# A cross network on one core: four staggered groups, batched tails and a row-major last layer in place of two interleaved groups

## The chip, the cores and the metric

The kernel runs on one core of a Trainium2 chip. That core has a matrix engine (TensorE, PE in the profile, with its weight loads as PEld), a vector engine (VectorE, DVE), a scalar engine (ScalarE, ACT), GpSimd (POOL), and SyncE (SP), which here only issues transfers to the core's 16 DMA engines. Matrix products land in PSUM (8 banks of 128 x 512 fp32); everything else lives in SBUF. The metric is the device time of one execution in microseconds. The kernel before was run three times: 513.07, 513.36 and 513.94 us, a median of 513.36.

## The reference

```python
B, F, D, L = 16384, 26, 16, 6
Din = min(F * D, 1024)            # 416
x = x0                            # x0: [16384, 416] bf16
for l in range(L):
    proj = jnp.einsum('bd,de->be', x, ws[l]) + bs[l]
    x = x0 * proj + x
return x
```

Six layers; each multiplies all 16384 rows by a 416 x 416 matrix, adds a bias, multiplies by the first input and adds the layer's input. The rows are independent of each other; the layers of one row follow each other.

## The kernel before, in words

**Layout.** The rows are cut into 8 groups of 2048 (`NG`, `GC`), a group into four chunks of 512 (`G_CH`, `CH`). Data is kept transposed: features on the partitions, rows along the free axis. 416 features are three tiles of 128 and a tail of 32. A group's three tiles are 128 x 2048 each; its tail is folded to 128 x 512, the four chunks below each other in strips of 32 partitions.

**One job** is one layer of one group. Its main tile i needs for each chunk three full products (128 x 128 weights, `emit_full`, L504) and one product of the 32 tail rows, which is row-tiled: four chunks at once in four strips of the array (`emit_k32`, L526 and L528). The tail of the output needs column-tiled products for the three main tiles (`emit_tail_cp`, L539, four chunks at once in four strips of 32 columns) and one 128 x 128 product with a block-diagonal weight `wbd` (`emit_tail_bd`, L559). In the order of a job the tile forms are full, rows, rows, full, full, rows, columns, block-diagonal. Tile 1 is begun with its row products and ended with its full ones (`k32_first`).

**Evacuation.** For each bank ACT adds the bias and writes bf16 to a staging tile `tmpw` (L420, 128 x 512). DVE multiplies a whole tile of 128 x 2048 by x0 (L738) and adds the old x (`emit_add`, L704), one addition held back behind the next multiply.

**Order.** `units` runs pairs of groups: groups 0 and 1 alternate through all six layers, then 2 and 3, and so on (`R = 2`). Each engine has its program written out by hand, with counters on semaphores. The first job of a layer waits for `sem_dve` of the same group's layer before, so that one other job lies between the two.

**Loads.** SP transposes x0 from DRAM into SBUF, three tiles and `Tbuf` for the tail, for each group (L238, L243, L253). For groups 2 to 7 a burst of four small products (`emit_x3init`, L485) copies the tail from `Tbuf` through PSUM into its folded form; groups 0 and 1 do that in their first job (L618).

**Outputs.** Groups 0 to 5 are written to a DRAM scratch `x6T` (L272, L275), transposed from there into `ost` (L296) and stored (L285). Groups 6 and 7 are transposed by PE at the end (L656, L658), copied out of PSUM by ACT (L449) and DVE (L773) and stored from SP (L346) and ACT (L436).

Of the kernel before, what the change touches and what calls it, by code (L numbers as in the profile page):

```python
# [3 lines left out]
P = 128  # L4
CH = 512

ACT_F = mybir.ActivationFunctionType
ALU = mybir.AluOpType
BF16 = mybir.dt.bfloat16
FP32 = mybir.dt.float32  # L10


def bass_standalone__cross_network_dcn__recsys_kernel(
# [8 lines left out]
    NMT = 3  # L22
    TAIL = D - NMT * P
    assert TAIL == 32, "kernel specialised for D = 416"
    Q = 4
    G_CH = 4
    GC = G_CH * CH
    assert B % GC == 0
    NG = B // GC
    R = 2 if NG % 2 == 0 else 1  # L30
    NR = NG // R
    NSLOT = 2 * R if NR > 1 else R
    KT = CH // P
    T0 = P - TAIL

    NBANK = 8
    NTW = 3
    NTS = 2
    NOST = 2
    GFIN = NG - 1  # L40
    TD_GROUPS = set(g for g in range(min(NG, 2)))
    N_WARM = 24

    x6T = nc.dram_tensor("x6T_scratch", [NG, D, GC], BF16, kind="Internal")

    wm = [[nc.alloc_sbuf_tensor(f"w_{l}_{t}", [P, D], BF16) for t in range(NMT)] for l in range(L)]
    w3 = [nc.alloc_sbuf_tensor(f"w3_{l}", [P, D], BF16) for l in range(L)]
    wbd = [nc.alloc_sbuf_tensor(f"wbd_{l}", [P, P], BF16) for l in range(L)]
    bias_bf = nc.alloc_sbuf_tensor("bias_bf", [P, 4, L], BF16)
    bias_f = nc.alloc_sbuf_tensor("bias_f", [P, 4, L], FP32)  # L50
    ident = nc.alloc_sbuf_tensor("ident", [P, P], BF16)
    x0T = [[nc.alloc_sbuf_tensor(f"x0T_{s}_{t}", [P, GC], BF16) for t in range(NMT)] for s in range(NSLOT)]
    x03 = [nc.alloc_sbuf_tensor(f"x03_{s}", [P, CH], BF16) for s in range(NSLOT)]
    xb = [[[nc.alloc_sbuf_tensor(f"x_{s}_{k}_{t}", [P, GC], BF16) for t in range(NMT)] for k in range(2)]
          for s in range(NSLOT)]
    xb3 = [[nc.alloc_sbuf_tensor(f"x3_{s}_{k}", [P, CH], BF16) for k in range(2)] for s in range(NSLOT)]
    Tb = nc.alloc_sbuf_tensor("Tbuf", [P, GC], BF16)
    tmpw = [nc.alloc_sbuf_tensor(f"tmpw_{i}", [P, GC], BF16) for i in range(NTW)]
    tmps = [nc.alloc_sbuf_tensor(f"tmps_{i}", [P, CH], BF16) for i in range(NTS)]
    ost = [nc.alloc_sbuf_tensor(f"ost_{i}", [P, KT, D], BF16) for i in range(NOST)]  # L60
    psum = nc.alloc_psum_tensor("ps", [P, NBANK * CH], FP32)

    sem_w = [nc.alloc_semaphore(f"sem_w{l}") for l in range(L)]
    sem_w0m = nc.alloc_semaphore("sem_w0m")
    sem_bias = nc.alloc_semaphore("sem_bias")
    sem_x0 = [nc.alloc_semaphore(f"sem_x0_{s}") for s in range(NSLOT)]
    sem_g0 = [nc.alloc_semaphore(f"sem_g0_{t}") for t in range(NMT)]
    sem_T = nc.alloc_semaphore("sem_T")
    sem_pe = nc.alloc_semaphore("sem_pe")
    sem_act = nc.alloc_semaphore("sem_act")  # L70
    sem_dve = nc.alloc_semaphore("sem_dve")
    sem_dm = nc.alloc_semaphore("sem_dm")
    sem_scr = nc.alloc_semaphore("sem_scr")
    sem_otr = [nc.alloc_semaphore(f"sem_otr{i}") for i in range(NOST)]
    sem_out = [nc.alloc_semaphore(f"sem_out{i}") for i in range(NOST)]
    sem_pool = nc.alloc_semaphore("sem_pool")
    sem_poolw = nc.alloc_semaphore("sem_poolw")
    sem_wbd = nc.alloc_semaphore("sem_wbd")
    sem_pet = nc.alloc_semaphore("sem_pet")
    sem_cpa = nc.alloc_semaphore("sem_cpa")  # L80
    sem_cpd = nc.alloc_semaphore("sem_cpd")
    sem_fin = nc.alloc_semaphore("sem_fin")
    sem_fin2 = nc.alloc_semaphore("sem_fin2")

    def slot_of(g):
        r, q = divmod(g, R)
        return (r % 2) * R + q if NR > 1 else q

    units = []
    for r in range(NR):  # L90
        for l in range(L):
            for q in range(R):
                g = r * R + q
                units.append(("job", g, l))
    for g in range(NG):
        if g in TD_GROUPS:
            continue
        idx = units.index(("job", g, 0))
        units.insert(max(idx - 1, 0), ("x3init", g, 0))

    banks = []
    eunits = []
    main_list = []
    small_list = []
    x3init_bank = {}
    x3init_eu = {}
    job_banks = {}
    job_eus = {}

    def add_eunit(kind, g, l, i, j, nb, ring, rk=None):  # L110
        eu = len(eunits)
        lst = main_list if ring == "w" else small_list
        if rk is None:
            rk = len(lst)
            lst.append(eu)
        else:
            lst[rk] = eu
        e = dict(kind=kind, g=g, l=l, i=i, j=j, first_bank=len(banks), last_bank=len(banks) + nb - 1,
                 ring=ring, rk=rk, ring_wait=(kind != "main1" or j == 0))
        eunits.append(e)  # L120
        return eu

    def add_x3init(g):
        eu = add_eunit("x3init", g, 0, None, None, 1, "s")
        x3init_bank[g] = len(banks)
        x3init_eu[g] = eu
        banks.append(dict(kind="x3init", g=g, l=0, i=None, j=0, eu=eu))

    for u in units:
        if u[0] == "x3init":  # L130
            add_x3init(u[1])
            continue
# [669 lines left out]
```

## Time and profile before

| what | value |
|---|---|
| runs | 513.07, 513.36, 513.94 us |
| span of the profiled execution | 511.6 us |
| its own device time beside the span | not listed apart; the median of the runs is 1.8 us above the span |
| mean granted TensorE clock | 0.995 |
| DMA | 53.91 MB in 134147 packets, mean 105 GB/s |
| ACT waiting for PE (L420 on L528) | 107.4 us in 96 waits |
| DVE waiting for ACT (L738 on L420) | 128.1 us in 95 waits |
| SP waiting for the output staging and scratch | 35.0 us on `out_dram<-ost`, 16.2 us on `ost<-x6T_scratch` |

The profile's page gives the busy time of each engine, then the span in 40 slices with the busy share in tenths, then the chain of work that ended last, and the costliest groups of instructions. A row of the timeline has the start in us, the length, the engine, the line of the kernel, the operation, output and inputs with their shapes, and the count of merged instructions. Matrix products are pipelined: each is listed with some 0.38 us although the next starts 0.22 us later, so spacings are read from starts, not from lengths. Tiles are named without their buffer numbers, so `x_1_0` stands for all tiles of that kind.

### The profile page before, as it was taken

Reading aid. Unit: us, or ns where it says so; the run is one execution under the profiler, and the core shown is the slowest. Engines: PE = TensorE matmul, PEld = TensorE weight load, DVE = VectorE, ACT = ScalarE, POOL = GpSimd, SP = SyncE. Lnnn points to the kernel's source line nnn. Section 1 sums busy time; section 2 is a strip of 40 time slices with the busy share of each in tenths; the row PEclk is TensorE's granted clock in tenths of the full one; section 3 lists DMA queues with packets and bytes.
Section 4 is the critical chain, followed back from the end, with each engine's and each line's share of the span. In section 5 each row is a group of like instructions: output and inputs, shape, how many; then the busy total and the mean of one; then the engine's idle time right before and its main releaser. Section 6 shows DMA issues by size and latency. Waiting matters only on the chain.

```text
span 511.6 us, 7778 instructions
## 1 busy us (share of the span) xinstructions
PE 485.9 (95%) x3069; PEld 198.8 (39%) x3118; DVE 376.9 (74%) x430; ACT 381.9 (75%) x646; POOL 9.5 (2%) x36
## 2 busy tenths in 40 slices
PE   5899999999999999999999999999999999999992
PEld 2333343343334334343433433343343343434352
DVE  0167787787788778778787877877887787787795
ACT  1467787787878778787877878787787777878782
POOL 1020200000000000000000000000000000000000
PEclk9999999999999999999999999999999999999998
DMA  9769700000667799000569579000277660000008
GB/s 168 153 150 206 142 2 0 1 1 1 176 168 233 159 209 190 1 0 2 163 156 247 136 200 215 15 2 1 57 218 217 184 168 0 1 1 0 1 2 266
DMA packets 134147, 53.91 MB, mean 105 GB/s; under 512 B 111584, under 2 KB 131808, under 8 KB 134112
## 3 DMA queue, kind: packets, MB, share of 16 engines
q1 hardware_dynamic: 128252, 51.29, 41.9%
q10 hardware_dynamic: 5860, 2.14, 1.8%
q8 instruction: 24, 0.39, 0.3%
q14 instruction: 11, 0.09, 0.0%
HBM read 2.56 MB, written 23.86 MB: 52 GB/s over the span
## 4 chain that ended last, share of the span: by engine, by line
PE 89%; DVE 3%; issue 2%; DMA 2%; ACT 2%; SPq 1%; DVEq 0%; ACTq 0%
PE ps L504 74%; PE ps L539 7%; PE ps L528 6%; PE ps L526 2%; DMA x0T_2<-in_x_dram 2%; ACT tmpw L420 2%; SPq L243 1%; DVE tmpw L743 1%; DVE x_0_1 L704 0%; PE ps L485 0%; DVE x_0_2 L704 0%; DVE x_1_1 L773 0%; DVE x_0_0 L704 0%; PE ps L656 0%; DVE tmpw L738 0%
## 5 line engine op out<-in xcount | busy, mean ns | idle before, releaser
L420 ACT ACTIVATE tmpw<-ps,bias_f 128x512 bf16<-128x512 f32 x576 | 343.7, 698 | 107.4 <-PE ps L528 107.4
L738 DVE TENSOR_TENSOR tmpw<-tmpw,x0T_2 128x2048 bf16<-128x2048 bf16 x47 | 57.6, 1225 | 51.9 <-ACT tmpw L420 51.9
L738 DVE TENSOR_TENSOR tmpw<-tmpw,x0T_1 128x2048 bf16<-128x2048 bf16 x47 | 57.6, 1226 | 48.2 <-ACT tmpw L420 48.2
L738 DVE TENSOR_TENSOR tmpw<-tmpw,x0T_0 128x2048 bf16<-128x2048 bf16 x47 | 57.3, 1219 | 28.6 <-ACT tmpw L420 28.1
L504 PE MATMUL ps<-x_1_0,w_0 128*128 128x512 bf16 x287 | 74.0, 380 | 3.3 <-issue 3.2
L504 PE MATMUL ps<-x_1_1,w_1 128*128 128x512 bf16 x288 | 73.9, 379 | 0.0
L504 PE MATMUL ps<-x_1_2,w_2 128*128 128x512 bf16 x288 | 73.9, 379 | 0.0
L504 PE MATMUL ps<-x_0_0,w_0 128*128 128x512 bf16 x192 | 49.4, 380 | 2.6 <-issue 2.6
L504 PE MATMUL ps<-x_0_1,w_1 128*128 128x512 bf16 x192 | 49.3, 379 | 0.0
L504 PE MATMUL ps<-x_0_2,w_2 128*128 128x512 bf16 x192 | 49.3, 379 | 0.0
L504 PEld LDWEIGHTS ps<-x_1_1,w_1 128*128 128x128 bf16 x288 | 28.2, 98 | 34.0
L504 PEld LDWEIGHTS ps<-x_1_2,w_2 128*128 128x128 bf16 x288 | 28.2, 98 | 34.0
L504 PEld LDWEIGHTS ps<-x_1_0,w_0 128*128 128x128 bf16 x288 | 25.9, 98 | 36.1 <-issue 10.2
L420 ACT ACTIVATE tmps<-ps,bias_f 128x512 bf16<-128x512 f32 x48 | 33.9, 705 | 0.0
L704 DVE TENSOR_TENSOR x_0_0<-tmpw,x_1_0 128x2048 bf16<-128x2048 bf16 (+1 forms) x27 | 29.7, 1099 | 0.0
L704 DVE TENSOR_TENSOR x_0_1<-tmpw,x_1_1 128x2048 bf16<-128x2048 bf16 (+1 forms) x27 | 29.7, 1099 | 0.0
L704 DVE TENSOR_TENSOR x_0_2<-tmpw,x_1_2 128x2048 bf16<-128x2048 bf16 (+1 forms) x27 | 29.7, 1099 | 0.0
L504 PE MATMUL ps<-x0T_0,w_0 128*128 128x512 bf16 x95 | 27.0, 402 | 2.8 <-DMA w_2<-in_ws_dram 1.4
L504 PE MATMUL ps<-x0T_1,w_1 128*128 128x512 bf16 x95 | 26.2, 399 | 3.2 <-DMA x0T_1<-in_x_dram 3.2
L504 PEld LDWEIGHTS ps<-x_0_2,w_2 128*128 128x128 bf16 x192 | 18.8, 98 | 22.7
L504 PEld LDWEIGHTS ps<-x_0_1,w_1 128*128 128x128 bf16 x192 | 18.8, 98 | 22.7
L504 PEld LDWEIGHTS ps<-x_0_0,w_0 128*128 128x128 bf16 x192 | 17.5, 98 | 23.8 <-issue 6.8
(204 smaller groups left out, 393.9 us busy)
## 6 DMA issues: line engine op xcount, KB each, us to landing
out_dram<-ost SPq DMA_DIRECT2D x25, 416.0 KB, 3.4
x6T_scratch<-x_0_0 SPq DMA_DIRECT2D x6, 512.0 KB
x6T_scratch<-x_0_1 SPq DMA_DIRECT2D x6, 512.0 KB
x6T_scratch<-x_0_2 SPq DMA_DIRECT2D x6, 512.0 KB
w_1<-in_ws_dram SPq DMA_DIRECT2D x6, 104.0 KB
w_2<-in_ws_dram SPq DMA_DIRECT2D x6, 104.0 KB
w_0<-in_ws_dram SPq DMA_DIRECT2D x5, 104.0 KB
out_dram<-x_1_0 SPq DMA_DIRECT2D x1, 416.0 KB, 2.7
```

The source lines that it names most:

```text
L243: sp.dma_start_transpose(x0T[s][t][:, :], x0[0:GC, t * P:(t + 1) * P]).then_inc(sem_g0[t], 16)
L420: act.activation(dst, src, ACT_F.Identity, bias=bias_ap, scale=1.0).then_inc(sem_act, 1)
L504: ins = pe.matmul(bank_ap(nb_of[(i, j)]), wm[l][t][:, ecols], xin[t][:, j * CH:(j + 1) * CH], start=(t == 0 and not k32_first), stop=last,)
L526: pe.matmul(bank_ap(nb_of[(i, j)]), lhsT, rhs, start=True, stop=False, tile_position=tp)
L528: pe.matmul(bank_ap(nb_of[(i, j)]), lhsT, rhs, start=False, stop=True, tile_position=tp).then_inc(sem_pe, 1)
L539: ins = pe.matmul(bank_ap(n, j * TAIL, (j + 1) * TAIL), wm[l][t][:, ecols], xin[t][:, j * CH:(j + 1) * CH], start=(t == 0 and not bd_first ...
L704: dve.tensor_tensor(o_ap, t_ap, i_ap, ALU.add).then_inc(sem_dve, 1)
L738: dve.tensor_tensor(tw[:, :], tw[:, :], x0T[s][i][:, :], ALU.mult).then_inc(sem_dm, 1)
L743: dve.tensor_tensor(tw[:, cols], tw[:, cols], x0T[s][i][:, cols], ALU.mult).then_inc(sem_dm, 1)
```

## The change

The kernel is written anew around a small recorder (`Program`): each instruction is added with the tiles that it reads and writes, and the recorder works out the semaphore waits. What is done on the chip changes in these parts:

- **Order.** A table `order` runs up to four groups at staggered layers: (0,5), (1,4), (2,3), (3,2), then (4,0), (1,5) and so on, as (group, layer). It ramps up from group 0 alone and down to group 7 alone.
- **Tiles in pairs.** Main tiles go in pairs: full products of one, its row products, the row products of the next, its full products. Pairs run across jobs.
- **Tails in batches.** Tails of up to four jobs are computed together (`cuts`, `tails`). The block-diagonal product becomes four column-tiled ones.
- **Evacuation.** ACT evicts two banks at once where they lie beside each other; DVE multiplies and adds halves of 1024 columns, adds right behind their multiplies.
- **Group 0** is loaded row-major by plain transfers and transposed by PE; the biases too. The other groups' tails reach their folded form by small transfers inside SBUF.
- **Outputs** of groups 0 to 6 are transposed by DMA from SBUF into `ost`, without the DRAM scratch.
- **The last layer of group 7** is computed row-major: x is the stationary operand and the weights move. Its x0 is loaded row-major beforehand (`load_last`), the layer's input is transposed by PE (`to_rows`), the bias is a product with a row of ones.

On PE, one steady job and a half of before, from the middle of the program. L504 are full products, L528 and L526 row products, L539 the column-tiled tail, L559 the block-diagonal product:

```order
303 L528 MATMUL ps<-x_2_1,w_3 128x512 x4
304 L539 MATMUL ps<-x_1_0,w_0 32x512 x4
305 L539 MATMUL ps<-x_1_1,w_1 32x512 x4
306 L539 MATMUL ps<-x_1_2,w_2 32x512 x4
307 L559 MATMUL ps<-x_2_1,wbd 128x512
308 L504 MATMUL ps<-x_1_0,w_0 128x512 x4
309 L504 MATMUL ps<-x_1_1,w_1 128x512 x4
310 L504 MATMUL ps<-x_1_2,w_2 128x512 x4
311 L528 MATMUL ps<-x_3_1,w_3 128x512 x4
312 L526 MATMUL ps<-x_3_1,w_3 128x512 x4
```

And of the changed kernel, with four tails in a row and the pairs behind them. L402 are full products, L414 row products, L427 and L432 the tail:

```order
129 L427 MATMUL ps<-x_4,wm 32x512 x12
130 L432 MATMUL ps<-x_4,wbd 32x512 x4
131 L427 MATMUL ps<-x,wm 32x512 x12
132 L432 MATMUL ps<-x_7,wbd 32x512 x4
137 L402 MATMUL ps<-x,wm 128x512 x12
138 L414 MATMUL ps<-x_7,w_5 128x512 x4
139 L414 MATMUL ps<-x_0,w_4 128x512 x4
140 L402 MATMUL ps<-x,wm 128x512 x24
141 L414 MATMUL ps<-x_0,w_4 128x512 x8
142 L402 MATMUL ps<-x,wm 128x512 x24
```

The column-tiled rows stood behind every third tile and now stand once in four jobs; between them twelve full products of one pair join the twelve of the next.

On SP, the output of group 0 before (DRAM scratch, then four transposes of a chunk each, with the stores between):

```order
36 L272 DMA x6T_scratch<-x_0_0 128x2048 [waits sem_dve]
37 L272 DMA x6T_scratch<-x_0_1 128x2048 [waits sem_dve]
38 L272 DMA x6T_scratch<-x_0_2 128x2048 [waits sem_dve]
39 L275 DMA x6T_scratch<-x_0_0 4x32x512 [waits sem_dve]
40 L296 DMA_TRANSPOSE ost<-x6T_scratch 128x4x416 [waits sem_scr]
41 L296 DMA_TRANSPOSE ost<-x6T_scratch 128x4x416
42 L285 DMA out_dram<-ost 128x4x416 [waits sem_otr0]
43 L296 DMA_TRANSPOSE ost<-x6T_scratch 128x4x416 [waits sem_otr0,sem_out0]
```

The output of group 1 in the changed kernel, and the loads of group 6 behind it:

```order
37 L524 DMA_TRANSPOSE ost<-x 128x16x128 [waits sem_out,sem_dve]
38 L524 DMA_TRANSPOSE ost<-x 128x16x128 [waits sem_dve] x2
39 L529 DMA_TRANSPOSE ost<-x_6 128x4x32 x4
40 L535 DMA out_dram<-ost 128x16x416 [waits sem_ot]
41 L295 DMA_TRANSPOSE x_1<-in_x_dram 128x2048 x3
42 L298 DMA_TRANSPOSE Tb<-in_x_dram 128x2048 [waits sem_x03_0]
```

Scratch writes and reads are gone; three large transposes and four small ones read from the x tiles in SBUF. On DVE, in the changed kernel, the first add that writes a set read by such a transpose (job (3,2), tile 0) waits for all seven:

```order
149 L370 TENSOR_TENSOR tw<-tw,x_2 128x1024 [waits sem_act] x2
150 L375 TENSOR_TENSOR x<-tw,x 128x1024 [waits sem_dve] x2
151 L370 TENSOR_TENSOR tw<-tw,x_3 128x1024 [waits sem_act] x2
152 L375 TENSOR_TENSOR x<-tw,x 128x1024 [waits sem_ot,sem_dve]
153 L375 TENSOR_TENSOR x<-tw,x 128x1024 [waits sem_dve]
```

Before, the x buffers of a slot alternated, and no add between two jobs waited on a transfer from SBUF; now six such adds do.

The diff, cut to its core:

```diff
-            for q in range(R):
-                g = r * R + q
-                units.append(("job", g, l))
+    NX0, NXS, NX3, NTW, NTS = 5, 6, 8, 4, 5
+    order = [(0, 0), (0, 1), (1, 0), (0, 2), (1, 1), (2, 0), (0, 3), (1, 2), (2, 1), (3, 0),
+             (0, 4), (1, 3), (2, 2), (3, 1), (0, 5), (1, 4), (2, 3), (3, 2), (4, 0), (1, 5),
+             (2, 4), (3, 3), (4, 1), (5, 0)]
+    order += [(NG - 1 - g, L - 1 - l) for g, l in reversed(order)]
+    cuts = [1, 2, 3, 4, 4, 4, 4, 4, 4, 4, 4, 4, 3, 2]
...
+    def load_group(g):
+        for t in range(NT):
+            add("sp", lambda h, t=t: h.dma_start_transpose(
+                x0s[s][:, t * GC:(t + 1) * GC], x0[rows, t * P:(t + 1) * P]), ...)
+        add("sp", lambda h: h.dma_start_transpose(Tb[:, :], x0[rows, D - P:D]), ...)
+        for j in range(NJ):
+            add("sp", lambda h, q=q, j=j: h.dma_start(x0s[s][q, XW:XW + CH], Tb[P - T32:P, j * CH:(j + 1) * CH]), ...)
...
+    def evacuate(g, l, i, banks, js, step):
+            add("act", lambda h, a=a, w=w, b0=b0: h.activation(
+                tw[r][:, a * CH:(a + w) * CH], psum[:, b0 * CH:(b0 + w) * CH], ACT_F.Identity,
+                bias=bias[:, i, l:l + 1], scale=1.0), ...)
+        for a in range(js[0], js[-1] + 1, step):
+            add("dve", ... ALU.mult), release=True)
+            add("dve", ... ALU.add), hold=True)
...
-                    pe.matmul(bank_ap(n), wbd[l][:, :], xin3[:, :], start=False, stop=True).then_inc(sem_pe, 1)
+    def tails(batch):
+        for (g, l), b in zip(batch, bs_):
+            for t in range(NT):
+                for j in range(NJ):
+                    add("pe", ... wm[l][:, t, NT * P:D], src(t, j, j + 1), tile_position=(0, j * T32))
+            for j in range(NJ):
+                add("pe", ... wbd[l][:, j * T32:(j + 1) * T32], s3, tile_position=(0, j * T32))
...
-                sp.dma_start(x6T[g, i * P:(i + 1) * P, :], xl[i][:, :]).then_inc(sem_scr, 16)
-                sp.dma_start_transpose(ost[os_][:, :, :], x6T[g, :, j * CH:(j + 1) * CH]).then_inc(sem_otr[os_], 16)
+    def output(g):
+        for t in range(NT):
+            add("sp", lambda h, t=t: h.dma_start_transpose(
+                ost[:, :, t * P:(t + 1) * P], xs[s][:, t * GC:(t + 1) * GC]), lane="ot", batch=g)
+        for j in range(NJ):
+            add("sp", lambda h, j=j, q=q: h.dma_start_transpose(
+                ost[:, j * KK:(j + 1) * KK, NT * P:D], x3s[s3][q, :]), lane="ot", batch=g)
+        add("sp", lambda h: h.dma_start(rows.rearrange(pat, **kw), ost...), lane="out", batch=g)
+        free_x.append(s)
...
+    def transposed_chunk(j):
+        for t in range(NT + 1):
+            for k in range(KK):
+                add("pe", ... h.transpose(psum_t(b)[:, c], x0n[:, j, k, t * P:(t + 1) * P], ident[:, :]))
+        for t in range(2):
+            add("act", ... x0s[s][:, cols(t, j)] from psum_t(ba))
+        add("dve", ... x0s[s][:, cols(2, j)] from psum_t(bb))
...
+    def nat_full(kk, j, b, first):
+        for t in range(NT):
+            add("pe", lambda h, t=t: h.matmul(bank(b, n=D), xcol(t, j, kk), wm[l][:, t, :], ...))
+    def nat_mul(kk, j, b):
+        add("act", lambda h: h.activation(o, bank(b, n=D), ACT_F.Copy), ...)
+        add("dve", lambda h: h.tensor_tensor(o, o, x0v, ALU.mult), ...)
+    def nat_store(kk, j0, j1, lane):
+        add("sp", lambda h: h.dma_start(dst, on[:, j0:j1, kk, :]), ...)
```

More of the change, by code (lines that the diff above doesn't have):

```diff
@@ L57, in bass_standalone__cross_network_dcn__recsys_kernel @@
[L57 to L65, printed above, removed]
@@ L777 @@
+    to_rows(1, bka)
+    for j in range(NJ):
+        nat_add(2, j)
+    nat_store(2, 0, NJ, "o7_2")
+    nat_rows(3, bkb, True)
+    for j in range(NJ):
+        nat_full(3, j, bkb[j], False)
+        nat_mul(3, j, bkb[j])
+        nat_add(3, j)
+        if j % 2 == 1:
+            nat_store(3, j - 1, j + 1, f"o7_3_{j}")
+    pr.emit()
 _INS = ['x0', 'ws', 'bs']
```

1287 lines of the change are left out of this document (611 added, 676 removed).

## The prediction

> **What bounds the kernel now.** I read the page's busy shares and slices first, then its chain of waits, then the timeline of PE for one steady job and for both ends.
>
> ```profile
> span 511.6 us, 7778 instructions
> PE 485.9 (95%) x3069; PEld 198.8 (39%) x3118; DVE 376.9 (74%) x430; ACT 381.9 (75%) x646; POOL 9.5 (2%) x36
> PE   5899999999999999999999999999999999999992
> PE 89%; DVE 3%; issue 2%; DMA 2%; ACT 2%; SPq 1%; DVEq 0%; ACTq 0%
> ```
>
> PE is busy in every slice but the first and the last, and 89% of the chain that ends last is PE. So time is gained by taking work or pauses from PE's stream, or by shortening the two ends. A stretch of PE's timeline (start, length, operation, count) shows one job of the steady state, group 3, layer 3:
>
> ```profile
> 207.06 0.39 PE L528 MATMUL ps<-x_2_1,w_3 32*128 32x512 bf16 x4
> 207.38 0.40 PE L539 MATMUL ps<-x_1_0,w_0 128*32 128x512 bf16 x4
> 207.61 0.39 PE L539 MATMUL ps<-x_1_1,w_1 128*32 128x512 bf16 x4
> 207.82 0.39 PE L539 MATMUL ps<-x_1_2,w_2 128*32 128x512 bf16 x4
> 208.37 1.03 PE L504 MATMUL ps<-x_1_0,w_0 128*128 128x512 bf16 x4 [0.16 <-issue]
> ...
> 211.06 0.40 PE L528 MATMUL ps<-x_3_1,w_3 32*128 32x512 bf16 x4
> 211.28 0.39 PE L526 MATMUL ps<-x_3_1,w_3 32*128 32x512 bf16 x4
> 211.60 1.04 PE L504 MATMUL ps<-x_1_0,w_0 128*128 128x512 bf16 x4
> ...
> 214.20 1.03 PE L504 MATMUL ps<-x_1_0,w_0 128*128 128x512 bf16 x4
> ...
> 216.89 0.39 PE L528 MATMUL ps<-x_3_1,w_3 32*128 32x512 bf16 x4
> ```
>
> A job lasts 216.89 - 207.06 = 9.83 us. The twelve full products of a tile take 214.20 - 211.60 = 2.60, or 0.217 each. A group of four row-tiled or column-tiled products (L526, L528, L539) takes about 0.22, as long as one full product. Each change between these forms costs about 0.1: full to rows 211.06 - 208.37 - 2.60 = 0.09, rows to full 211.60 - 211.28 - 0.22 = 0.10. The pure products of a job are 3 x 2.60 + 3 x 0.217 + 4 x 0.217 = 9.32, so 0.51 us of each job are changes of form.
>
> **The change, part by part.** The same two windows split the span: first job up to 27.53, the other 47, and the output of the last two groups.
>
> ```profile
> 27.53:495.16 467.63, 459.20 (x2854) 184.82 (x2899) 362.93 (x394) 366.43 (x618) 7.11 (x20) 1.00 0.41 99
> 495.16:511.60 16.44, 7.08 (x128) 6.05 (x127) 10.34 (x34) 7.11 (x16) 0.00 (x0) 0.86 0.65 208
> ```
>
> *Steady state.* Tiles now come in pairs full, rows, rows, full. That stands in the trace already: from 208.37 to 214.20, 5.83 us for two tiles with both changes of form, 2.915 a tile. A tail costs four groups of four, 4 x 0.217 = 0.87, because the block-diagonal product is now four column-tiled ones beside each other; a batch of tails adds two changes, 0.2. After the first tile 140 tiles, 47 tails and 14 batches remain: 140 x 2.915 + 47 x 0.87 + 14 x 0.2 = 451.8. The six bursts that copied the 32 tail rows of later groups through PSUM go. One of them shows here:
>
> ```profile
> 128.33 0.39 PE L539 MATMUL ps<-x_1_2,w_2 128*32 128x512 bf16 x4
> 128.97 0.40 PE L485 MATMUL ps<-Tbuf,ident 32*32 32x512 bf16 x4 [0.25 <-issue]
> 129.30 1.04 PE L504 MATMUL ps<-x_1_0,w_0 128*128 128x512 bf16 x4
> ```
>
> From the last column group to the next full product pass 0.97 us here and 0.55 at 207.82: 0.42 saved six times, which the 451.8 has by leaving them out.
>
> *What must hide beside it.* ACT evicts two banks at once, DVE multiplies and adds halves of 1024 columns. Neither shape is in the trace, so I bound them by the spacing of the shapes that are:
>
> ```profile
> 484.44 2.42 ACT L420 ACTIVATE tmpw<-ps,bias_f 128x512 bf16<-128x512 f32 x4 [1.09 <-PE ps L528]
> 488.44 4.74 ACT L420 ACTIVATE tmpw<-ps,bias_f 128x512 bf16<-128x512 f32 x8 [1.00 <-PE ps L528]
> 488.04 1.22 DVE L704 TENSOR_TENSOR x_0_1<-tmpw,x_1_1 128x2048 bf16<-128x2048 bf16 x1
> 489.18 0.42 DVE L749 TENSOR_TENSOR tmps<-tmps,x_2 128x512 bf16<-128x512 bf16 x1
> 489.51 1.22 DVE L704 TENSOR_TENSOR x_0_2<-tmpw,x_1_2 128x2048 bf16<-128x2048 bf16 x1
> 490.65 0.42 DVE L704 TENSOR_TENSOR x_2_0<-tmps,x_2_1 128x512 bf16<-128x512 bf16 x1
> ```
>
> ACT: 4.74 / 8 = 0.59 for 512 columns, so 1024 lie between 0.59 and 1.19; I take 1.15. DVE starts 1.14 apart on 2048 and 0.33 apart on 512, so 1024 lie between 0.57 and 0.67; I take 0.60. For four jobs (PE 4 x 3 x 2.915 + 4 x 0.87 + 0.2 = 38.7) ACT needs 24 x 1.15 + 4 x 0.59 = 30.0 (30.9 at most) and DVE 48 x 0.60 + 8 x 0.33 = 31.4 (34.8 at most). Both stay hidden behind PE. The tightest place is the second bank set: its last pair is free about 2.4 us after its tile, PE's next rows want it after 2.69 + 0.22 = 2.9. If an eviction took 1.4, those 0.5 us would be gone and PE would pause at each pair.
>
> *Waits that are added.* A job's predecessor lies three jobs back (some 29 us), so the old wait on DVE between jobs stays covered. In the ramp it isn't: group 0 layer 1 stands right behind layer 0. There two evictions, then four small ones with a multiply and an add each, end about 1.5 us after PE wants the last chunk. Taken: 1.5 (0 to 3).
>
> A new wait is DVE's on the output transposes (`sem_ot`). Only six x sets exist, and an output set is written again one to two jobs after its last tile (six times, for groups 0 to 5). Counted in tiles of 2.915 from the first finished tile of that group to the first add that waits, DMA has 23 to 34 us, about 27, for three large and four small transposes from SBUF. All later multiplies and adds stand behind a waiting add; ACT runs out of its four staging buffers four tiles later, and PE out of banks. No row shows an SBUF source; these are the nearest:
>
> ```profile
> x0T_0<-in_x_dram SPq DMA_TRANSPOSE x8, 4.9
> ost<-x6T_scratch SPq DMA_TRANSPOSE x24, 3.8
> out_dram<-ost SPq DMA_DIRECT2D x25, 416.0 KB, 3.4
> L238 SPq DMA_TRANSPOSE x0T_0<-in_x_dram x7: 2257/2567/3137, 12.3 to 308.9; - x7
> ```
>
> A transpose of the same 512 KB from DRAM holds SP for 2.6 us and lands after 4.9. I take that: 3 x 2.6 + 4 x 0.6 + 4 = 14 of the 27 us, hidden; bounds 1.4 to 3.1 a piece. Behind it in SP stand the store and the loads of group g+5, wanted some 70 us later. Early on SP issues group 0's loads, two weight loads and group 1's transposes in turn: 4 x 0.5 + 2 + 4 x 2.6 + 5 lands them by 20, wanted at about 33.
>
> [...]
>
> *Start.* Four products took 1.89 us at 5.71 and 1.03 at 18.93: the array ran at half rate till then, and PE waited twice for a transposed load.
>
> ```profile
> 5.71 1.89 PE L504 MATMUL ps<-x0T_0,w_0 128*128 128x512 bf16 x4 [1.43 <-DMA w_2<-in_ws_dram]
> 10.78 1.89 PE L504 MATMUL ps<-x0T_1,w_1 128*128 128x512 bf16 x4 [3.19 <-DMA x0T_1<-in_x_dram]
> 13.89 1.89 PE L504 MATMUL ps<-x0T_2,w_2 128*128 128x512 bf16 x4 [1.23 <-DMA x0T_2<-in_x_dram]
> 18.93 1.03 PE L504 MATMUL ps<-x0T_2,w_2 128*128 128x512 bf16 x4
> 495.16 0.61 PE L656 MATMUL ps<-ident,x_0_0 128*128 128x128 bf16 x8 [0.16 <-issue]
> ```
>
> Now four plain loads of 416 KB arrive, the first about 0.7 + 4 = 4.7 us in. Each chunk then needs 16 PE transposes (0.06 each at full rate by the row at 495.16, 0.11 at half: 0.9 to 1.7 us) and three products (0.65 to 1.3), with ACT's two copies of about 0.63 each beside them. With a wait of 0.4 for the copies a warm chunk is 2.0, a cold one 3.1 with hardly any. Four chunks end at 4.7 + 4 x 2.0 = 12.7 warm and 4.7 + 4 x 3.1 = 17.1 cold. I take 16.0 with what is left of half rate behind it (13 to 18.5).
>
> [...]
>
> *End.* The last layer of group 7 is computed row-major: x is the stationary operand, loaded with a stride of four elements; w moves, 416 columns, 0.217 x 416 / 512 = 0.176. Four passes of twelve such, two row groups and two changes: 4 x (2.11 + 0.35 + 0.2) = 10.7. Two blocks of 24 transposes and 8 small ones: 2 x 1.8 = 3.6. PE ends at T + 14.3, T being the end of the last regular tile (group 6's third). A contiguous weight load takes 98 ns; strided I take the same; above 176 it would show, and at 390 it would add 10 us.
>
> ```profile
> L504 PEld LDWEIGHTS ps<-x_1_1,w_1 128*128 128x128 bf16 x288 | 28.2, 98 | 34.0
> L449 ACT ACTIVATE x_1_0<-ps 128x416 bf16<-128x416 bf16 x4 | 1.8, 557 | 0.0
> 498.93 0.37 SPq L346 DMA_DIRECT2D out_dram<-x_1_0  x1
> 506.28 1.15 ACTq L436 DMA_DIRECT2D out_dram<-tmpw  x1
> out_dram<-tmpw ACTq DMA_DIRECT2D x1, 416.0 KB, 4.8
> ```
>
> Behind PE come one multiply, one add and a store that lands in 3.4 to 4.8: T + 20.3. The other path: group 6's third tile is ready at T + 3.6, its transposes have landed by T + 11, and then 3.4 MB (group 6, then group 7) must be stored through SP. In the old kernel the same eight stores went from 498.93 to 506.28 + 4.8 = 511.1, 1.5 us each: T + 11 + 12.2 = T + 23. I take T + 22 (19 to 28).
>
> **Sum.** 16.0 + 451.8 + 1.5 + 22 = 491.3 for the span. The median of the runs shown, 513.36, lies 1.8 above the profiled span of 511.6; I add it: **493 us**, 4% less. The gain is about 8 from the tails and pairs, 2.5 from the six bursts, the rest from the two ends.
>
> **Rivals.** *Slow SBUF transposes (slower than before).* If a large one takes t, an output needs 3.3 t against 27 us; what is missing stops DVE, then PE, at six reuses of a set, and the end grows by 3.3 t - 8. The gain of 20 is used up from t = 8.2: 6 x 0.1 + 19. At t = 10 it is 6 x 6 + 25 = 61: 554. For it: no row has an SBUF source. Against it: DRAM sources take 2.6, a third of the deciding value.
>
> *Evictions bind.* If 1024 columns cost 1.4 or more, or DVE's order holds a buffer, PE pauses 0.15 us or so at 70 pairs: 10 us, 503. Against it: spacing of 0.59 a bank.
>
> *A slow end.* Strided weights at 390 ns, or stores that queue: T + 32, 503.
>
> *The change doesn't do what it says:* the pairs cost as much per tile as before, only the ends and the bursts gain: 501. Against it: the pair stands in the trace with 5.83.
>
> **How the numbers follow.** Forecast 0.76 (484 to 501: start 13 to 18.5, stall 0 to 3, end 19 to 28); evictions 0.06, slow end 0.07, no gain in pairs 0.03, slow transposes 0.08. A range of 484 to 507 takes in all but the last and the forecast's edges. Faster by over 0.2% (about what a measurement can tell from no change): 0.92, all but the slow transposes; these split into 0.01 within and 0.07 slower.
>
> **What would show it.** PE's timeline: 5.83 for a pair, 3.5 for four tails, no pause on ACT between. DVE's waits: no time on the output transposes; if there is, the first rival. First tile done at 16 us; the last stores leave some 22 us behind group 6's third tile. Wrong would be a PE idle above 5 us in total between 40 and 460, or a large transpose above 8 us.

## The result, and the profile after

The changed kernel takes **498.57 us** (median of 496.72, 497.07, 500.08 and 500.27), the kernel before 513.28 beside it: ratio 0.9715, 95% interval 0.9683 to 0.9748, faster by 2.9%. The forecast was 493.0, the range 484 to 507. The profiled execution is the one of 500.08 us; its span is 498.3, so 1.8 us lie around it, as before. One execution of experiment e6 (627.72 us, mean granted clock 0.752) was in a slower state and is left out of all that follows.

The page of the changed kernel: span, busy shares, the slices of PE and of the granted clock, and the chain that ended last.

```profile
span 498.3 us, 8040 instructions
PE 474.5 (95%) x3197; PEld 204.5 (41%) x3251; DVE 405.4 (81%) x710; ACT 343.0 (69%) x371; POOL 9.6 (2%) x37
PE   6999999999999999999999999999999999999990
PEclk8899999999999999999999999999999999999996
PE 89%; DVE 4%; issue 2%; DMA 2%; ACT 1%; ACTq 0%
```

PE is still the bound, with the same 95% and the same 89% of the chain; it has 11.4 us less to do (485.9 before). What is new is the last slice of PE: 0. For the last 12.5 us PE does nothing; DVE finishes in the first 3 us of them, and behind that only transfers run.

Two windows split the span at the first tail (18.20) and at T, the first product of the row-major last layer (472.17). The columns are the length, then PE, PEld, DVE, ACT and POOL busy, the granted clock, the share of DMA and GB/s.

```profile
18.20:472.17 453.97, 447.30 (x2944) 185.64 (x2993) 386.59 (x660) 325.70 (x340) 6.46 (x19) 1.00 0.40 87
472.17:498.30 26.13, 13.62 (x148) 8.79 (x144) 15.53 (x43) 11.61 (x21) 0.00 (x0) 0.85 0.57 156
```

Against the prediction's sum:

| term | forecast | measured |
|---|---|---|
| start, to the end of the first tile | 16.0 | 18.2 |
| middle, with the stall in the ramp | 451.8 + 1.5 = 453.3 | 453.97 |
| end, from T | 22 | 26.1 |
| span | 491.3 | 498.3 |

The middle is 0.7 off, 0.15%. The two ends miss by 2.2 and 4.1 in this execution; it is one of the two long ones.

**Middle.** PE's timeline of the changed kernel, two pairs and what a batch of tails costs (L402 full, L414 rows, L427 and L432 tails):

```profile
52.30 0.61 PE L414 MATMUL ps<-x,w 32*128 32x512 bf16 x8
52.84 5.35 PE L402 MATMUL ps<-x,wm 128*128 128x512 bf16 x23
58.13 0.39 PE L414 MATMUL ps<-x,w 32*128 32x512 bf16 x4
58.45 0.83 PE L427 MATMUL ps<-x,wm 128*32 128x512 bf16 x12
59.33 0.82 PE L427 MATMUL ps<-x,wm 128*32 128x512 bf16 x12
...
63.86 0.61 PE L414 MATMUL ps<-x,w 32*128 32x512 bf16 x8
64.40 5.35 PE L402 MATMUL ps<-x,wm 128*128 128x512 bf16 x24
69.69 0.61 PE L414 MATMUL ps<-x,w 32*128 32x512 bf16 x8
```

A pair takes 69.69 - 63.86 = 5.83, a tail 59.33 - 58.45 = 0.88, as forecast to 0.01. PE's list of waits says the same: beside the wait for the identity at the start (1.8) and the rows below it holds nothing over 0.4 us.

```profile
PE ps L402 <- issue: 3.7, 23, 0.2
PE ps L402 <- DMA w<-in_ws_dram: 2.8, 1, 2.8
PE ps L402 <- DVE x L375: 1.0, 3, 0.4
```

Total us, times, longest. The wait on DVE's adds, with 0.4 more on the add of a tail, is the stall in the ramp: 1.4 for 1.5. There is no row in which DVE waits for the output transposes.

**Start.** The chain of waits and PE's timeline for the first 18 us:

```profile
1.80 8.34 DMA w<-in_ws_dram
```

```profile
4.75 1.41 PE L483 MATMUL ps<-ident,x 128*128 128x128 bf16 x12
6.69 0.84 PE L483 MATMUL ps<-ident,x 128*128 128x128 bf16 x12
10.65 1.06 PE L402 MATMUL ps<-x,wm 128*128 128x512 bf16 x2 [2.79 <-DMA w<-in_ws_dram]
11.50 1.49 PE L483 MATMUL ps<-ident,x 128*128 128x128 bf16 x12
13.46 1.46 PE L402 MATMUL ps<-x,wm 128*128 128x512 bf16 x3
18.20 0.83 PE L427 MATMUL ps<-x,wm 128*32 128x512 bf16 x12
```

The first chunk is there at 4.75, as forecast. The second chunk's twelve transposes run at full rate (0.84). Then PE stands 2.8 us for the weights of layer 0, which were on their way for 8.3 us, and behind that wait it is back at half rate (1.49 for the same twelve; 3 products in 1.46).

**End.** SP's timeline from the third tile of group 6 on (L524 large and L529 small transposes of group 6, L535 its store, L740 those of group 7), and the windows of the stores:

```profile
476.41 3.09 SPq L524 DMA_TRANSPOSE ost<-x  x1
479.54 5.08 SPq L529 DMA_TRANSPOSE ost<-x  x4
485.76 0.37 SPq L535 DMA_DIRECT2D out_dram<-ost  x1
486.18 7.58 SPq L740 DMA_DIRECT2D out_dram<-x  x5
```

```profile
476.00:486.00 10.00, 9.79 (x113) 6.65 (x111) 9.63 (x30) 8.41 (x17) 0.00 (x0) 1.00 0.42 68
486.00:492.00 6.00, 0.00 (x0) 0.00 (x0) 2.68 (x8) 0.06 (x1) 0.00 (x0) 0.89 0.90 288
492.00:498.30 6.30, 0.00 (x0) 0.00 (x0) 0.00 (x0) 0.00 (x0) 0.00 (x0) 0.50 0.84 267
```

While PE works on its last 10 us DMA moves 68 GB/s; all of 3.4 MB leaves in the 12.5 us after 485.76, when PE is done.

### The profile page after: what moved, and what is told of

Same layout as the page of the kernel before. It is cut to its first block, busy times and chain, and to the rows that moved or that the text cites. A ratio compares the mean times of both kernels' runs of the same rounds, so it can differ in the third digit from the quotient of the medians.

```text
span 498.3 us, 8040 instructions
## 1 busy us (share of the span) xinstructions
PE 474.5 (95%) x3197; PEld 204.5 (41%) x3251; DVE 405.4 (81%) x710; ACT 343.0 (69%) x371; POOL 9.6 (2%) x37
## 4 chain that ended last, share of the span: by engine, by line
PE 89%; DVE 4%; issue 2%; DMA 2%; ACT 1%; ACTq 0%
PE ps L402 72%; PE ps L414 8%; PE ps L427 6%; PE ps L432 2%; DMA w<-in_ws_dram 2%; ACT tw L361 1%; DVE x L735 1%; DVE x L375 1%; PE ps L700 1%; DVE tw L370 1%; PE ps L483 1%; DVE x L695 0%; DVE x L730 0%; PE ps L675 0%; PE ps L488 0%
## 5 line engine op out<-in xcount | busy, mean ns | idle before, releaser
L361 ACT ACTIVATE tw<-ps,bias 128x1024 bf16<-128x1024 f32 (+1 forms) x295 | 300.6, 1074 | 129.7 <-PE ps L414 106.4
L402 PE MATMUL ps<-x,wm 128*128 128x512 bf16 x1638 | 373.7, 380 | 9.1 <-issue 3.7
L370 DVE TENSOR_TENSOR tw<-tw,x 128x1024 bf16<-128x1024 bf16 (+1 forms) x286 | 194.1, 683 | 68.7 <-ACT tw L361 68.2
L402 PEld LDWEIGHTS ps<-x,wm 128*128 128x128 bf16 x1692 | 159.0, 98 | 218.5 <-issue 31.3
L375 DVE TENSOR_TENSOR x<-tw,x 128x1024 bf16<-128x1024 bf16 (+1 forms) x286 | 182.0, 677 | 0.0
L414 PE MATMUL ps<-x,w 32*128 32x512 bf16 x564 | 44.5, 380 | 0.4 <-DVE x L392 0.4
L427 PE MATMUL ps<-x,wm 128*32 128x512 bf16 x564 | 38.7, 380 | 0.0
L388 ACT ACTIVATE ts<-ps,bias 128x512 bf16<-128x512 f32 x47 | 28.8, 701 | 0.0
L414 PEld LDWEIGHTS ps<-x,w 32*128 32x128 bf16 x564 | 9.0, 92 | 33.5 <-issue 32.4
L427 PEld LDWEIGHTS ps<-x,wm 128*32 128x32 bf16 x564 | 13.8, 96 | 15.5 <-issue 3.2
L392 DVE TENSOR_TENSOR x<-ts,x 128x512 bf16<-128x512 bf16 x47 | 18.6, 418 | 0.0
L390 DVE TENSOR_TENSOR ts<-ts,x 128x512 bf16<-128x512 bf16 x47 | 18.6, 418 | 0.0
L432 PE MATMUL ps<-x,wbd 128*32 128x512 bf16 x188 | 18.3, 379 | 0.0
L432 PEld LDWEIGHTS ps<-x,wbd 128*32 128x32 bf16 x188 | 5.0, 97 | 5.1
L735 DVE TENSOR_TENSOR x<-x,x 128x416 bf16<-128x416 bf16 x16 | 5.1, 369 | 0.1
```

The source lines that it names most:

```text
L361: add("act", lambda h, a=a, w=w, b0=b0: h.activation(tw[r][:, a * CH:(a + w) * CH], psum[:, b0 * CH:(b0 + w) * CH], ACT_F.Identity, bias=b ...
L370: add("dve", lambda h, a=a, e=e: h.tensor_tensor(tw[r][:, a * CH:e * CH], tw[r][:, a * CH:e * CH], x0s[s0][:, i * GC + a * CH:i * GC + e * ...
L375: add("dve", lambda h, a=a, e=e: h.tensor_tensor(xs[so][:, i * GC + a * CH:i * GC + e * CH], tw[r][:, a * CH:e * CH], src(i, a, e), ALU.ad ...
L388: add("act", lambda h: h.activation(ts[r][:, :], bank(b), ACT_F.Identity, bias=bias[:, 3, l:l + 1], scale=1.0), reads=[("ps", b), "bias"], ...
L390: add("dve", lambda h: h.tensor_tensor(ts[r][:, :], ts[r][:, :], x0s[s0][:, XW:XW + CH], ALU.mult), reads=[("ts", r)] + x03_toks(s0), writ ...
L392: add("dve", lambda h: h.tensor_tensor(x3s[so][:, :], ts[r][:, :], src, ALU.add), reads=[("ts", r)] + stok, writes=[("x3", so)], hold=True)
```

## The experiments

For each profiled run three lengths are read: start (to the first tail), middle (to the first product of the last layer) and end (to the end of the span).

| run | start | middle | end | median us | ratio to before |
|---|---|---|---|---|---|
| changed kernel | 18.20 | 453.97 | 26.1 | 498.57 | 0.9715 (0.9683 to 0.9748) |
| e1 tails singly | 18.53 | 460.68 | 25.5 | 504.91 | 0.9835 (0.9805 to 0.9866) |
| e8 no pairs | 15.17 | 466.95 | 25.3 | 511.19 | 0.9971 (0.9951 to 0.9991) |
| e5 whole tiles on DVE | 15.42 | 455.14 | 26.4 | 501.92 | 0.9766 (0.9734 to 0.9798) |
| e2 group 0 by DMA | 18.16 | 453.96 | 26.7 | 500.55 | 0.9751 (0.9733 to 0.9769) |
| e3 weights first | 13.75 | 453.96 | 25.4 | 496.09 | 0.9677 (0.9655 to 0.9699) |
| e4 small ones first | 17.01 | 453.97 | 21.0 | 494.25 | 0.964 (0.9613 to 0.9667) |
| e7 = e3 + e4 | 13.99 | 453.97 | 21.0 | 490.78 | 0.9574 (0.9555 to 0.9593) |
| e9 = e7 + e5 | 15.39 | 455.14 | 21.6 | 493.02 | 0.9608 (0.9587 to 0.963) |
| e10 = e7, outputs twice | 15.81 | 453.96 | 21.3 | 492.32 | 0.9582 (0.9558 to 0.9607) |
| e11 PE kept busy | 15.23 | 453.97 | 25.3 | 496.81 | 0.9679 (0.9645 to 0.9713) |
| e12 = e7, store in two | 13.77 | 453.97 | 19.2 | 489.53 | 0.9544 (0.9504 to 0.9585) |

The middle is the same to 0.01 us wherever PE's order and DVE's pieces are left alone. The profiled executions of these kernels differ at their ends alone. For the other executions no stage is on record.

### What the batches and the pairs are worth (e1, e8)

e1 computes each job's tail by itself:

```diff
-    cuts = [1, 2, 3, 4, 4, 4, 4, 4, 4, 4, 4, 4, 3, 2]
+    cuts = [1] * 47
```

> Every tail is computed alone behind the first tile of its own job; products and bytes are those of the changed kernel, but PE changes its form 241 times in place of 175. Theory A (PE's stream is the bound, a change of form costs 0.1 us): 66 more changes, 6 to 7 us more than the changed kernel's 498.6, so 505. Rival B (the gain comes from DVE's finer steps and the longer distance between dependent layers, forms cost nothing): 498 to 500.

e8 keeps the batches and gives every tile the form full, rows:

```diff
+    for n in list(mode):
+        mode[n] = "F1"
```

> Every main tile is full products and then its row products; no tile begins with its rows, so PE changes form 301 times in place of 175. Theory A: 126 x 0.1 = 12 to 13 us more, 511, nearly all of the gain gone. Rival B: 498 to 500. With the run of single tails this gives two points of the price per change; if it is no straight line, waits on banks come in as well.

Measured: 504.91 and 511.19; both expectations held. Each change of form has a price, and the two edits add a known number of them, counted in PE's order: 175 in the changed kernel, 241 in e1, 301 in e8. The middle grows by 460.68 - 453.97 = 6.71 for 66, and by 12.98 for 126: **0.102 and 0.103 us a change**. In PE's timeline of e8 a tile is seen with both of its changes:

```profile
202.21 2.76 PE L402 MATMUL ps<-x,wm 128*128 128x512 bf16 x12
204.91 0.40 PE L414 MATMUL ps<-x,w 32*128 32x512 bf16 x4
205.24 2.76 PE L402 MATMUL ps<-x,wm 128*128 128x512 bf16 x11
```

From start to start 3.03 us a tile, where a paired tile takes 2.915.

How much of the gain over the kernel before is this? Its block-diagonal product has the shape of a full one. In PE's weight loads of before, the two stand behind each other:

```profile
208.14 0.10 PEld L559 LDWEIGHTS ps<-x_2_1,wbd 128*128 128x128 bf16 x1 [0.42 <-issue]
208.16 0.53 PEld L504 LDWEIGHTS ps<-x_1_0,w_0 128*128 128x128 bf16 x3
```

The next full product starts at 208.37, 0.55 behind the third column group at 207.82. That is two products of 0.217 and one change, so the step from the block-diagonal product to the full ones costs none. A job of before has five changes, which are the 0.51 us of the prediction. Counted like this, PE changes form 250 times between 27.53 and 495.16 in the kernel before, 12 of them at the six bursts, and 168 times (of the 175) between 18.20 and 472.17 in the changed kernel. Without the bursts 70 are saved, and 70 x 0.103 = 7.2 us of the 13.3 by which the span fell. The bursts, 0.42 each, are another 2.5. The first job ends 2.4 earlier: at 27.53 before, now at 18.20 + 0.87 + 0.2 + 5.83 = 25.1. That leaves 1.2 us without a name. These shares are worked out from the traces and the price of a change; they are no runs of their own.

The kernel without pairs is within 0.3% of the kernel before, but it isn't the old order: with two changes a tile it has some 44 more changes than the kernel before (294 between its windows), about 4.5 us, and makes up for them elsewhere, at the bursts and the start above all.

### What the halves on DVE are worth (e5, e9)

DVE multiplies and adds 2048 columns at a time, ACT unchanged:

```diff
-        step = 1 if fine and i == NT - 1 else 2
+        step = 1 if fine and i == NT - 1 else 4
```

> DVE multiplies and adds whole tiles of 2048 columns as the old kernel did, not halves. Theory A: DVE's busy time falls by about 25 us (405 to 380) and the time doesn't move (497 to 500), because PE never waits for it in the steady state. Rival B: the later results delay dependent products, 3 us or more.

Measured 501.92, with executions from 499.2 to 502.33. That missed the expectation and by the median reached the 3 us of rival B, but the changed kernel has two clusters of its own (497 and 500), so the median did not say whether DVE or the start was at fault. e9 repeats the edit on e7, whose executions lie within 0.8 us:

> The kernel with both ends mended (490.78), and DVE multiplying and adding whole tiles of 2048 columns where it took halves of 1024. Theory: the halves are not what keeps PE fed. DVE stays some 80 us behind PE in busy time, no job waits for it but the two in the ramp, so the time stays within 1.5 us: 489.5 to 492.3, DVE busy about 392 where it was 405. Rival: whole tiles hand x to the next job too late and PE pauses on DVE: 494 or more, with over 3 us of PE waiting for DVE's adds.

Measured 493.02 (492.45 to 494.25): above what the theory allowed, below the rival. The middle decides: 455.14 in both, 1.17 us more than with halves. PE's waits in e9, where the kernel with halves has 1.0 and 0.3:

```profile
PE ps L402 <- DVE x L375: 1.5, 3, 1.0
PE ps L414 <- DVE x L392: 0.9, 1, 0.9
```

So halves are worth 1.2 us, all of it in the ramp, where a job follows its own predecessor. In the steady state they save nothing: behind 60 us PE waits for DVE in neither kernel. DVE is busy for 392.1 us instead of 405.4. The profiled execution of e9 is its longest, 3.1 us of span above e7's; the other 1.9 us lie in its start (15.39 for 13.99) and end (21.6 for 21.0). At its start PE still worked at half rate in the second chunk:

```profile
7.59 1.46 PE L484 MATMUL ps<-ident,x 128*128 128x128 bf16 x12 [0.53 <-DMA x<-in_x_dram]
```

In e7 the same twelve transposes took 0.84.

### The start (e2, e3, e6, e11)

e2 loads group 0 like the others, by transposes from DRAM, with no PE transposes:

```diff
-    for j in range(NJ):
-        add("sp", lambda h, j=j: h.dma_start(x0n[:, j, :, :], perm(g0, j)), ...)
+    load_group(0)
...
-                transposed_chunk(0)
...
-                for j in range(1, NJ):
-                    transposed_chunk(j)
-                    full(g, l, i, banks, True, True, chunks=[j - 1])
-                full(g, l, i, banks, True, True, chunks=[NJ - 1])
+                full(g, l, i, banks, True, False)
```

> Group 0 is loaded by transposing transfers like the other groups, no PE transposes. Theory A with the start as it was seen (first tile done at 18 us, 2.8 of it waiting for the weights): the third transposed load lands at 14 and the row products need the tail's copy at about 18, so the first tile ends at 19 to 22 and the total is 1 to 4 us higher, 500 to 503. Rival: PE's transposes are worth the full 10 us that separate the old first job from the new one, 508.

Measured 500.55 (500.49 to 500.7). PE waits 6.9 us for x and then has half rate (twelve products in 4.71), and the first tail starts at 18.16: no later than in the profiled execution of the changed kernel. As it stands, transposing group 0 on PE brings 2 us by the medians, and next to nothing beside the two executions at 500: PE is then stopped by the weights instead of by x. e3 takes that stop away: layer 0's weights go out on SP behind the first chunk.

```diff
     for j in range(NJ):
         add("sp", lambda h, j=j: h.dma_start(x0n[:, j, :, :], perm(g0, j)), ...)
+        if j == 0:
+            load_w(0, "sp")
...
-    load_w(0, "act")
```

> The weights of layer 0 are issued from SP right behind the first chunk of group 0, the other three chunks behind them. If the start was late because the weights shared the transfer engines with four chunks (they landed at 10.1 us, PE waited 2.8 us and fell back to half rate), they land at about 6, the first tile ends at 13.5 to 15.5 in place of 18, and the total is 2.5 to 4 us lower, 495. If PE's half rate has its own clock and the transposes and copies set the pace, only the 1 us or so is gained: 497.5.

Measured 496.09 (494.88 to 497.13). PE's timeline of e3, to set beside that of the changed kernel:

```profile
7.42 0.84 PE L484 MATMUL ps<-ident,x 128*128 128x128 bf16 x12 [0.36 <-DMA x<-in_x_dram]
8.75 0.59 PE L402 MATMUL ps<-x,wm 128*128 128x512 bf16 x2 [0.16 <-ACT x L494]
10.27 0.82 PE L402 MATMUL ps<-x,wm 128*128 128x512 bf16 x3
12.02 1.47 PE L402 MATMUL ps<-x,wm 128*128 128x512 bf16 x6
13.75 0.83 PE L427 MATMUL ps<-x,wm 128*32 128x512 bf16 x12
```

No wait for weights, full rate from 7.42 on (0.82 for three products, 1.46 before), the first tail 4.45 us earlier. The median is 2.5 us lower, as expected. How much of that is the half rate? e6 puts 56 products of the identity with itself where PE waits, so that the array has work:

```diff
                     transposed_chunk(j)
+                    if j == 1:
+                        for _ in range(56):
+                            add("pe", lambda h: h.matmul(psum[:, 7 * CH:7 * CH + P], ident[:, :], ident[:, :],
+                                                         start=True, stop=True), ...)
                     full(g, l, i, banks, True, True, chunks=[j - 1])
```

> 56 small products (128 columns) are put in front of the first full product, where PE waits for the weights, so that PE isn't idle there. If the idle gap sends PE back to half rate for the next 5 us, the two kinds of runs (497 and 500) become one at 496 to 497, and the products behind the gap start 0.22 us apart. If the half rate there doesn't come from the gap, nothing changes or it is 1 us longer, since 56 products at half rate take 6 us in place of the 2.8 of the gap.

Measured 497.78 to 499.08, ratio 0.9717 (0.9697 to 0.9738): no gain, a miss. The four executions are one cluster, as expected, but it lies at 498 instead of 496 to 497. No timeline of these four is on record. By count the 56 products, 0.06 each, end about 0.5 us after the weights, which is not all of the difference. e11 has 42:

> The changed kernel with 42 products of the identity with itself (0.06 us each, 2.5 us) where PE waits 2.8 us for the first layer's weights; fewer than the 56 before, so that they end when the weights land. Theory: an idle PE is what brings the half rate back, and that is the 3 us between the executions at 497 and those at 500. Then the spread falls below 1.5 us and all lie at 496.0 to 497.5. Rival: the half rate has another cause; then executions at 500 remain.

Measured 496.81 (496.4 to 498.18): the median as expected, the spread 1.8 instead of under 1.5, and no execution at 500. PE's timeline of e11:

```profile
7.11 2.52 PE L640 MATMUL ps<-ident 128*128 128x128 bf16 x42
10.01 0.82 PE L402 MATMUL ps<-x,wm 128*128 128x512 bf16 x3 [0.38 <-DMA w<-in_ws_dram]
15.23 0.83 PE L427 MATMUL ps<-x,wm 128*32 128x512 bf16 x12
```

The weights land little earlier (10.01 for 10.65), but the array is at full rate when they do, and the first tail starts at 15.23. Of the 4.45 us between the changed kernel's profiled start and e3, the half rate behind the wait is 18.20 - 15.23 = 3.0 and the wait itself the other 1.5. The 3.0 are near the 3.3 between the two clusters of the changed kernel, and the mean granted clock agrees: 0.985 and 0.986 in the two long executions, 0.990 and 0.991 in the two short ones. That the half rate makes the clusters is likely by this, but only one of the four has a timeline, and four executions of e11 without one at 500 can be chance. Why the half rate comes back in some executions and not in others is open: e5 and e8 waited 2.7 and 2.8 us for the weights as well and stayed at full rate (first tails at 15.42 and 15.17).

### The end (e4, e7, e12)

e4 issues the small transposes of group 6 ahead of its third large one; their source is ready before that tile:

```diff
-        for t in range(NT):
+        def big(t):
             add("sp", lambda h, t=t: h.dma_start_transpose(
                 ost[:, :, t * P:(t + 1) * P], xs[s][:, t * GC:(t + 1) * GC]), ...)
+
+        for t in range(NT - 1):
+            big(t)
+        if g != LAST - 1:
+            big(NT - 1)
         for j in range(NJ):
             add("sp", ... ost[:, j * KK:(j + 1) * KK, NT * P:D], x3s[s3][q, :])
+        if g == LAST - 1:
+            big(NT - 1)
```

> The four small output transposes of group 6 are issued ahead of its third large one; they were ready 9 us earlier. If the end is set by the stores, which start when SP has issued these small ones (5.1 us for four), group 6's store starts at 481 in place of 485.8 and the span ends 3.5 to 4.5 us earlier, total 494.5. If DVE's last multiply and add set the end, 0 to 1 us: 498.

Measured 494.25 (492.03 to 496.22), the end 21.0 instead of 26.1: the five us of SP for four small transposes had stood between the last tile and all stores. e7 has both e3 and e4:

> Weights first (as e3) and small transposes first (as e4) together. If both causes are right and independent, their gains add: 6 to 8 us below 498.6, so 491 to 492.5. If the end is bound elsewhere, no better than the better one of the two.

Measured 490.78, and all four executions within 490.75 and 491.5; the gains add, a little past the 491 to 492.5 that were expected, and it beats both kernels. That the wait for the weights was the only source of clusters does not follow: e3 has no such wait either, and its six executions lie at 494.9 to 495.2 and at 497.0 to 497.1. What makes e3's second cluster is open. SP's timeline of e7 at the end, and the window of the stores:

```profile
472.20 1.62 SPq L525 DMA_TRANSPOSE ost<-x  x1
476.46 0.38 SPq L543 DMA_DIRECT2D out_dram<-ost  x1
477.22 7.79 SPq L748 DMA_DIRECT2D out_dram<-x  x5
```

```profile
480.00:485.00 5.00, 1.57 (x9) 0.80 (x7) 4.47 (x13) 1.85 (x4) 0.00 (x0) 1.00 1.05 336
```

The stores still begin at T + 8.5 and then fill the DMA engines (share 1.05, 336 GB/s). e12 stores the first 256 columns of group 6 as soon as two large transposes have landed:

```diff
...
+        if last:
+            store(0, 2 * P, [("ost", t) for t in range(NT - 1)], "outa")
+            big(NT - 1, "ot2")
+            store(2 * P, D, [("ost", NT - 1)] + [("ost", NT, j) for j in range(NJ)], "out")
```

> The kernel with both ends mended (490.78), and the store of group 6 cut in two: columns 0 to 255 once the first two large transposes have landed, the other 160 at the end. Theory: the stores of the end are bound by bandwidth from 476.4 on (3.4 MB in some 12 us), and 1.05 MB now go while PE still computes group 6's third tile; the path through PE, the last add (484.6) and a store that lands in some 4 binds instead: 489.0 to 490.5. Rival: pieces of 512 and 320 bytes move so much slower than rows of 832 that the gain is lost: 491 or more.

Measured 489.53 (488.73 to 491.39), as the theory had it: the early store goes out at 467.43, the end is 19.2 instead of 21.0. The medians of e12 and e7 stem from different chips, and the ranges touch; the length of the end is what shows the gain.

### The cover of the output transposes (e10)

e10 issues the three large output transposes of groups 0 to 5 a second time, on e7:

```diff
+        else:
+            for t in range(NT):
+                big(t, "ot2")
```

> The kernel with both ends mended (490.78), and the three large output transposes of groups 0 to 5 issued a second time behind the four small ones (the same data to the same place). Each output then takes some 11 us more: a wait for the small ones, 3 x 2.0 on SP and 4.6 to land. In the kernel with both ends mended 7 to 13 us pass between the last transpose of an output and the first add that waits for it. Theory: of the six adds two to four wait, 1 to 5 us each, ACT's staging buffers take that up and PE loses at most 3 us: 490.5 to 494. Rival: the wait passes on to DVE and PE at once and the cover is smaller than read: 6 x 5 to 6 x 11 us more, 520 to 555.

Measured 492.32 (490.91 to 492.94). SP's timeline of e10, the output of group 1 (two rounds of large ones), and DVE's only wait on it:

```profile
204.85 11.61 SPq L525 DMA_TRANSPOSE ost<-x  x3
216.50 5.73 SPq L535 DMA_TRANSPOSE ost<-x  x4
224.97 7.85 SPq L525 DMA_TRANSPOSE ost<-x  x3
234.43 0.39 SPq L546 DMA_DIRECT2D out_dram<-ost  x1
```

```profile
DVE x L375 <- DMA ost<-x: 1.0, 1, 1.0
```

The output now takes 29.6 us (20.1 in e7, 203.05 to 223.16). Four of the other five take 24.2 to 25.6; for the sixth no length is on record. Of six adds one waits, 1.0 us, just for this longest output, and PE's middle is 453.96: nothing is passed on. The rival fell, and even the theory had expected more waits. The profiled span is 2.1 us above e7's: 1.8 in the start (15.81), where PE waited 1.8 us for the second chunk and had half rate behind it (twelve transposes in 1.35), and 0.3 in the end; none in what was doubled. (A wait of this kind is not wholly new: in the kernel before DVE waited for the scratch writes of an earlier group at L735, though its list of waits shows no time there.)

## Why the prediction was right, and where it was off

**The middle was right, for the stated reason.** Pairs at 5.83, tails at 0.87, changes of form at about 0.1 gave 453.3 for 453.97, and e1 and e8 show the price of a change as 0.102 and 0.103. What was said to hide beside it hid. Two evictions of 1024 columns by ACT take 2.12 us in the steady state, so about 1.06 each (1.15 taken, 1.4 would have bound); two additions of 1024 by DVE 1.28 with a length of 0.69 each, so 0.59 apart (0.60 taken). The rivals *evictions bind* and *the change doesn't do what it says* fell. Of the gain, the prediction gave about 8 us to tails and pairs and 2.5 to the bursts, where 7.2 and 2.5 are found. It gave the rest, some 10, to the two ends. They brought 2.4, all of it at the start: the end of 26.1 holds a job of some 9.7 us, and the 16.4 that remain are those of the kernel before (16.44).

**Slow SBUF transposes** fell as well. The large ones held SP for 1.96 us in the median and landed after 4.6 (2.6 and 4.9 taken); the last row has the small ones, 1.24 for the 0.6 taken:

```profile
L524 SPq DMA_TRANSPOSE ost<-x x21: 1524/1964/3093, 159.9 to 476.4; - x21
DMA to landing us min/median/max: 4.2/4.6/5.9
...
L529 SPq DMA_TRANSPOSE ost<-x x28: 1162/1239/1961, 170.0 to 483.4; - x28
```

The cover of about 27 us was sized about right: in e10 an output of 29.6 us made an add wait for 1.0, four of 24.2 to 25.6 made none wait, and PE lost nothing.

**The start: the wait for the weights was left out.** The prediction worked out the chunks from transposes, products and copies, 2.0 us warm and 3.1 cold, and let the weights be there. The chunks were as stated: 12.02 - 10.27 = 1.75 warm in e3, and 14.72 - 11.50 = 3.2 cold in the changed kernel. But 416 KB of weights, issued on ACT's queue beside four chunks of x0, another set of weights and group 1's first transposes, took 8.3 us to land (DMA share 1.16, 313 GB/s from 1.80 to 10.14), and behind that wait the half rate was back. 18.2 instead of 16.0 came of both together: with the wait alone the start is 15.2 to 15.4 (e5, e8), below the 16.0. With the wait gone it is 13.75, 0.7 above the warm sum of 12.7 and 0.33 for the row products. The 18.5 at the top of the range for the start was the author's estimate of a start at half rate throughout; no run shows such a start. Here twelve transposes took 0.84 at 6.69, and e3 kept full rate from 7.42 on with transposes as more than half of PE's work. That 18.2 is near 18.5 is chance; the half rate came back behind a wait. In e9, on the other hand, transposes were PE's main work from 4.75 on and the half rate lasted until 10.8. No run here leaves out the 28 products ahead of them, so what those do for PE's rate is not shown.

**The end: the small transposes were sized at half their price.** The prediction let group 6's transposes land by T + 11; its store began at T + 13.6. The third tile was ready at T + 4.2 (3.6 taken), its transpose took 3.1 (2.6), the four small ones 5.08 (4 x 0.6 = 2.4), the landing behind them 1.1 (2.4 is what remains of the predicted 11): together 2.6 later. The stores then took 12.5 for 12.2, so T + 26.1 where the steps had T + 23 and 22 was taken; the "taken" lay below the worked-out path for no reason, and cost one more us. What the strided weight loads might have added did not come: the first twelve products with them took 2.23 us with a change of form (472.17 to 474.40), where 2.11 and 0.1 were taken; such a load took 115 ns in the mean, 98 were taken.

Both misses are of one sign, which is why the time came out 5.6 us above the forecast, though inside the range, whose upper half was made of just these two ends. Where in the range it fell is in part luck: executions at 497 and at 500 came up twice each.

## What to carry to other kernels

Where PE is the bound and its work comes in several tile shapes, count the changes between them: here each costs 0.10 us, 70 fewer of them are over half of the gain, and the count foretold the middle of the new order to 0.15%. Check first which steps are changes at all: two products that do different work can have the same shape. Price the first and the last 20 us with the same care, with each transfer that they wait for and its place in the queue: moving two groups of issues there brought 7.8 us by the medians, over half as much as the whole change. And compare runs by stage: when the middle agrees to 0.01 us, a start that varies by 3 us no longer hides what an edit does there.

## What the runs showed of the hardware that was not expected

- Half rate came back behind a short pause of PE, for 3 to 5.5 us, in some of the profiled executions only: after waits of 2.8 us (changed kernel), 2.9 (e1), 3.2 (e4) and 1.8 (e10), but not after 2.7 and 2.8 us (e5, e8). In e4 the two products behind the wait still ran at full rate (0.59), half rate began about 1 us later. In the changed kernel the granted clock showed it, 0.50 in the window from 10 to 15 us. The half rate of the first products (28 in 3.17 us, 0.11 each; 0.06 in e11's 42) stood beside a granted clock of 1.00, and how long that first half rate lasts varies: the first twelve transposes at 4.6 to 4.8 us took 0.83 in e4, e10 and e11, and in e9 it lasted until 10.8. What decides it was not shown.
- A transpose of 32 KB from SBUF held SP for 1.24 us in the median, over half of the 1.96 of one of 512 KB, with a sixteenth of the bytes.
- 416 KB of weights took 8.3 us to land while other transfers filled the DMA engines (share 1.16, 313 GB/s).
